# A layer norm's last step moves from ScalarE to POOL, and the negated DFT tables from POOL to ScalarE and VectorE

## The chip, the cores and the metric

The kernel runs on one core of a Trainium2 chip. The metric is device time in microseconds of one execution; the kernel before takes 612.58 us, the median of nine runs that lie between 611.94 and 614.32. A core has five engines that run side by side, each with a queue of its own that it works through in order: TensorE (PE: matmuls; PEld is its loading of weights), VectorE (DVE), ScalarE (ACT), GpSimd (POOL) and SyncE (SP). POOL and SP also issue the transfers (DMAs). An instruction waits at the head of its engine's queue until what it needs is there, and all that stands behind it waits too.

## The reference

Eight batches of attention without softmax (12 heads, 448 positions, 64 columns a head), whose output is the input of a block that mixes with a Fourier transform over positions and columns, normalises, and runs a feed-forward of 768 to 3072 to 768:

```python
scores = scale * np.matmul(q, k.transpose(0, 1, 3, 2))
attn = np.maximum(scores, 0.0) ** 2 / S
x = np.matmul(attn, v)                      # then (B, S, H * D)
X = np.fft.fft(np.fft.fft(x, axis=1), axis=2)
u = x + np.real(X)
un = (u - mean(u)) / np.sqrt(var(u) + 1e-06)     # over the last axis
out = u + np.maximum(un @ w_ch1, 0.0) @ w_ch2
```

## The kernel before

The program writes out every instruction in an order that it plans itself: each piece of work is a generator that yields `need(engine, duration, dependencies, buffers)`, and `Streams.run` (line 79) always takes the piece that could start first by these planned durations. What an instruction is planned to cost, and on which engine, therefore decides the order on all five queues. The hardware then follows that order, with waits on what is really done.

Loading. POOL issues all loads of q, k, v and the weights (lines 306, 335, 345). All matmuls take bf16.

Attention of a batch (line 492): 24 score tiles of 112 x 896 in six groups of four, one group for each pair of heads. A tile's scores are two matmuls (line 544) into one of three double PSUM buffers; ACT takes the relu (line 564) and so frees the buffer; VectorE squares it (line 570); after four tiles TensorE multiplies them with v (line 530, eight matmuls, called the attention values here). `fold` (line 445) copies the result to `xT` (lines 451 to 458) and makes its sum and difference with its mirror image (lines 466, 467). In the start one of the three double PSUM buffers is held for batch 0's channel transform.

Tables. `build_dft` (line 250) makes cosine and sine tables in the first 25 us: VectorE works out a fraction of a turn in three operations (lines 256 to 258, in `turns`), and ACT takes the sine (line 262, in `sine`). `seq` is the table over positions, `chan` three tables over columns. Batch 0 also needs negated ones: `nseq`, the negative of the sine half of `seq`, and `chan_neg`, of a part of each `chan`. `negate` (line 244) makes these four on POOL, planned for 18 us or later.

Start. Batch 0 has no feed-forward beside it. Its channel transform (`first_channels`, line 951, matmuls in line 963) waits in the plan for the folds, the tables and all four `negs_ready`. In the gaps TensorE gets fillers on a tile of zeros (line 1136, `warming`). After the last fold come the copy in line 1000, batch 0's position transform (line 611, where `nseq` is used), its norm and the first feed-forward.

From batch 1 on, three streams are interleaved: the feed-forward of one batch (line 1096 with a relu on ACT in line 1069, then line 1114 with an add on VectorE in line 1077), the attention of a later one, and the mix between them. The position matmuls of a mix (line 838) come in two chunks of rows. `mix_rows` (line 830) handles a chunk: a copy on ACT (line 844), sum and difference on VectorE (line 849), two tiles `u`, one on POOL and one on VectorE (lines 858, 859), their storing, statistics on VectorE (lines 870, 871), a root on ACT (line 874), `rstd` and `nmr` on VectorE (lines 877, 879), and for each of the two tiles `un` = `u` x `rstd` + `nmr` on ACT (line 884). From batch 2 on `un` is stored to DRAM, one tile by SP (`ntop`, line 903) and one by POOL (`nbot`, line 906), and read back transposed (line 929, `unT`) for the feed-forward. So a batch has four `un`, and the six batches from 2 on have 24.

Of the kernel before, what the change touches and what calls it, by code (L numbers as in the profile page):

```python
# [113 lines left out]
def need(eng, dur, deps=(), bufs=(), ok=None):  # L114
    return eng, dur, list(deps), list(bufs), ok
# [6 lines left out]
def act(n):  # L122
    return n / 1200 + 0.2
# [14 lines left out]
def kernel(  # L138
# [24 lines left out]
    SX = 240  # L163
# [75 lines left out]
    chan_neg = work.tile([128, 3, 2, KH], BF16, name="channeg", tag="xn", bufs=1)  # L239
    dft_ready, indices_ready = Cell(), Cell()  # L240

    negs_ready = [Cell() for _ in range(4)]

    def negate(dst, src, t):

        e = yield need("POOL", 0.55, [t, 18.0])
        nc.gpsimd.tensor_scalar(dst, src, -1.0, None, op0=ALU.mult)
        [c for c in negs_ready if c.t is None][0].t = e + LATENCY["POOL"]

    def build_dft():  # L250
        row, col, col2 = drow, dcol, dcol2

        def turns(f, g, cols, rows, n, i):

            r = work.tile([128, 2 * KH], mybir.dt.int32, name="dftr", tag=f"pc{TC[i][0]}", bufs=1)
            nc.vector.tensor_scalar(r[:, :n], cols, rows, None, op0=ALU.mult)
            nc.vector.scalar_tensor_tensor(f, cols, rows, r[:, :n], op0=ALU.mult, op1=ALU.subtract)
            nc.vector.scalar_tensor_tensor(g, f, -1.0, f, op0=ALU.mult, op1=ALU.max)

        def sine(dst, y, n, e, sign=1, bias=zero_t):  # L260
            e = yield need("ACT", act(n), [e + LATENCY["DVE"]])
            nc.scalar.activation(dst, y, AF.Sin, bias=bias, scale=sign * 2.0 * math.pi)
            dft_ready.t = e + LATENCY["ACT"]

        e = yield need("DVE", 0.3, [indices_ready])
        nc.vector.tensor_scalar(row[:, 0:2], row[:, 0:2], 1.0 / S, None, op0=ALU.mult)
        nc.vector.tensor_scalar(row[:, 4:7], row[:, 4:7], 1.0 / D, None, op0=ALU.mult)

        e = yield need("DVE", 2.1, [indices_ready])
        f = work.tile([128, 4 * KH], FP32, name="dfty", tag="u", bufs=2)  # L270
        g = work.tile([128, 4 * KH], FP32, name="dfty", tag="u", bufs=2)
        for i in range(2):
            turns(f[:, i * SX:(i + 1) * SX], g[:, i * SX:(i + 1) * SX], col[:, 0:SX], row[:, i:i + 1], SX, i)
        yield from sine(seq[:, 0, :, :].rearrange("p a s -> p (a s)"), g[:, :2 * SX], 2 * SX, e, -1, halfpi)
        yield from sine(seq[:, 1, :, :].rearrange("p a s -> p (a s)"), f[:, :2 * SX], 2 * SX, e)
        sch.add(negate(nseq, seq[:, 1], dft_ready.t), (1, 1))

        for m in range(3):
            e = yield need("DVE", 1.5, [indices_ready])
            y = work.tile([128, 4 * KH], FP32, name="dfty", tag="u1" if m < 2 else "o", bufs=2)  # L280
            turns(y[:, 2 * KH:], y[:, 0:2 * KH], col2, row[:, 4 + m:5 + m], 2 * KH, m % 2)
            yield from sine(chan[m][:, 0, :], y[:, 0:2 * KH], 2 * KH, e, -1, halfpi)
            yield from sine(chan[m][:, 1, :], y[:, 2 * KH:], 2 * KH, e)
            sch.add(negate(chan_neg[:, m], chan[m][:, :, KH:], dft_ready.t), (1, 1))


    GRP = 4 * R * HG * Dh * 4
# [542 lines left out]
    def mix_rows(b, ch, pcs):  # L830
# [48 lines left out]
        nc.vector.scalar_tensor_tensor(nmr[:n], mv[:n, :, 0], -1.0, rstd[:n],  # L879
                                       op0=ALU.mult, op1=ALU.mult)  # L880
        for i, u in enumerate(us):
            e = yield need("ACT", act(D), [e + (LATENCY["DVE"] if i == 0 else 0.0)])
            un = work.tile([128, D], BF16, name="un", tag=f"un{2 * ch + i}", bufs=1)
            nc.scalar.activation(un[:n], u[:n], AF.Identity, bias=nmr[:n, i:i + 1],  # L884
                                 scale=rstd[:n, i:i + 1])
            uns[b][2 * ch + i] = un
            freed[i].t = e
            if b == 1:
                nr, idn, c0, w = ((128, ident, 64, 128), (128, rev[:, 0:127], 64 + HS + 97, 127),
                                 (96, ident[:96, :96], 64 + 128, 96), (97, rev[:97, 31:128], 64 + HS, 97))[2 * ch + i]  # L890
                sch.add(turn_rows(un, e + 1.5, nr, idn, c0, w, ("DVE", "ACT")[i],
                                  second_un[1 + 2 * ch + i]), (1, 1))
# [58 lines left out]
    def first_channels(i, ms):  # L951

        n0, n1 = TC[i]
        for m in ms:
            e = yield need("PE", 4 * mm(KH), [f_ready[m], dft_ready] + negs_ready + ([first_scores] if i else []),
                           [BS] if i and m == 0 else [])
            if i and m == 0:
                first_pps[i] = BS.take()
            for t in range(2):
                parts = [(0, 2 * KH, chan[m][:, t, :])] if m < 3 else \  # L960
                    [(0, KH, chan[m - 3][:, t, 0:KH]), (KH, 2 * KH, chan_neg[:, m - 3, t, :])]
                for c0, c1, tab in parts:
                    nc.tensor.matmul(first_pps[i][:n1 - n0, t, c0:c1], lhsT=first_folds[m][:, t, n0:n1], rhs=tab,  # L963
                                     start=(i == 1 and m == 0), stop=(m == MC - 1 and c1 == 2 * KH))
# [221 lines left out]
```

## Time and profile before

| | |
|---|---|
| median of nine runs | 612.58 us (611.94 to 614.32) |
| profiled execution, its own time | 614.71 us |
| its span, first to last instruction | 612.7 us |
| mean granted TensorE clock | 0.994 |
| TensorE busy in 0 to 60 us | 53.65 us |
| TensorE busy in 60 to 612.7 us | 545.95 us |
| POOL line 247, nseq / chan_neg | 1.83 / 1.19 to 1.22 us |
| ACT line 884, un, mean of 28 | 1.02 us |
| POOL line 688, the same step for two tiles of batch 0 | 0.98 us |

A line of a timeline gives the start in us, the time in us, the engine, the source line, the operation, what it writes and reads with shapes, how many instructions were merged, and in brackets how long the engine had been idle before and what ended that. A line of the busy table gives a stretch and the busy time of PE, PEld, DVE, ACT and POOL in it with their counts, then the granted TensorE clock, the DMA share and GB/s. In the row of slices each digit is one fortieth of the span, in tenths.

### The profile page before, as it was taken

How to read it: one execution, taken by the hardware profiler on the slowest of the kernel's cores; microseconds unless marked ns; L12 is line 12 of the kernel's file. 1: busy time of each engine (PE TensorE's matmuls, PEld its weight loads, DVE VectorE, ACT ScalarE, POOL GpSimd, SP SyncE). 2: the span in 40 equal slices, each digit the busy share in tenths (PEclk: the TensorE clock that was granted, in tenths of full speed). 3: DMA queues.
4: the chain of work that ended last, by engine and by line, in shares of the span. 5: the costliest groups of instructions: out<-in, count | busy, mean ns of one | idle time of the engine just before them, and what ended most of it. 6: DMA issues, size and time to landing. Idle time of an engine off the chain costs nothing.

```text
span 612.7 us, 10252 instructions
## 1 busy us (share of the span) xinstructions
PE 599.6 (98%) x4048; PEld 331.3 (54%) x4067; DVE 333.3 (54%) x764; ACT 315.6 (52%) x469; POOL 132.4 (22%) x179
## 2 busy tenths in 40 slices
PE   9898999999999999999999999999999999999997
PEld 6556555644455565555445555555445565554464
DVE  6967686864677769545743468645733447110011
ACT  5656763387646468535773167634781346104300
POOL 8823031420242115211420114210410004000000
PEclk9889999999999999999999999999999999999999
DMA  9999999956947994987475774887462225420022
GB/s 125 207 197 200 225 174 127 183 122 110 141 109 182 206 166 160 156 169 122 158 136 105 147 125 158 160 155 116 135 136 70 86 50 170 98 102 26 0 78 78
DMA packets 125216, 82.22 MB, mean 134 GB/s; under 512 B 76272, under 2 KB 113168, under 8 KB 125168
## 3 DMA queue, kind: packets, MB, share of 16 engines
q0 software_dynamic: 40320, 34.07, 35.9%
q1 hardware_dynamic: 84848, 47.50, 31.9%
q8 instruction: 32, 0.52, 0.4%
q14 instruction: 16, 0.13, 0.1%
HBM read 62.91 MB, written 26.69 MB: 146 GB/s over the span
## 4 chain that ended last, share of the span: by engine, by line
PE 86%; DVE 6%; ACT 4%; issue 1%; DMA 1%; POOL 0%; SPq 0%; DVEq 0%; ACTq 0%; POOLq 0%
PE psF L1114 36%; PE psF L1096 32%; PE psS L544 7%; PE psF L530 7%; PE psS L988 2%; ACT sq L564 2%; DMA qkT<-qkr 1%; PE psS L838 1%; ACT un L884 1%; DVE sq L570 1%; PE psS L963 1%; PE psS L1136 1%; DVE stats L870 1%; ACT hT L1069 0%; DVE stats L635 0%
## 5 line engine op out<-in xcount | busy, mean ns | idle before, releaser
L1096 PE MATMUL psF<-unT,w 128*128 128x384 bf16 (+1 forms) x1134 | 227.5, 352 | 2.2 <-ACT hT L1069 1.1
L564 ACT ACTIVATE sq<-psS 112x896 bf16<-112x896 f32 x192 | 165.5, 916 | 118.5 <-PE psS L544 118.5
L1114 PE MATMUL psF<-w,hT 128*128 128x384 bf16 (+2 forms) x1343 | 224.8, 326 | 0.1
L1114 PEld LDWEIGHTS <-hT 128*128 128x128 bf16 x1344 | 129.3, 98 | 92.4 <-issue 8.8
L1096 PEld LDWEIGHTS <-w 128*128 128x128 bf16 x1152 | 109.3, 98 | 111.1 <-issue 14.7
L1069 ACT ACTIVATE hT<-psF 128x512 bf16<-128x512 f32 (+1 forms) x180 | 98.3, 548 | 97.3 <-PE psF L1096 96.3
L570 DVE TENSOR_TENSOR sq<-sq 112x896 bf16<-112x896 bf16 x192 | 117.0, 624 | 49.9 <-ACT sq L564 48.3
L1077 DVE TENSOR_TENSOR o<-psF,o 128x384 f32<-128x384 f32 (+2 forms) x56 | 31.0, 554 | 108.9 <-PE psF L1114 108.4
L451 DVE TENSOR_SCALAR xT<-psF 128x224 bf16<-128x224 f32 x48 | 18.7, 391 | 75.4 <-PE psF L530 71.1
L544 PE MATMUL psS<-qkT 64*112 64x448 bf16 x384 | 53.4, 371 | 1.3 <-ACT sq L564 1.2
L306 POOL DMA_DIRECT2D vn<-in_v_dram x24 | 17.2, 719 | 172.1 <-PE psF L530 153.9
L530 PE MATMUL psF<-sq,vn 112*64 112x448 bf16 x384 | 46.2, 363 | 0.7 <-ACT hT L1069 0.5
L858 POOL TENSOR_TENSOR u<-tp,xn 128x385 f32<-128x385 f32 (+1 forms) x14 | 17.3, 1237 | 105.1 <-DVE tp L849 91.6
L544 PEld LDWEIGHTS <-qkT 64*112 64x112 bf16 x384 | 20.9, 126 | 28.9 <-issue 24.4
L884 ACT ACTIVATE un<-u,nmr,rstd 128x768 bf16<-128x768 f32 (+1 forms) x28 | 28.2, 1021 | 6.7 <-DVE nmr L879 5.6
L530 PEld LDWEIGHTS <-vn 112*64 112x64 bf16 x384 | 18.3, 110 | 22.9 <-issue 14.5
L870 DVE BATCH_NORM_STATS2 stats<-u 128x6 f32<-128x384 f32 (+1 forms) x56 | 28.1, 539 | 0.0
L906 POOL DMA_INDIRECT ubot<-u,back x16 | 16.4, 1028 | 39.6 <-DVE hT L1067 25.0
L1136 PE MATMUL psS<-warm 128*128 128x126 bf16 (+1 forms) x214 | 20.1, 248 | 1.3 <-DVE warm L215 1.3
L306 POOL DMA_DIRECT2D qn<-in_q_dram x21 | 15.4, 732 | 27.3 <-PE psF L427 11.0
L906 POOL DMA_INDIRECT nbot<-un,back x12 | 11.7, 975 | 38.0 <-ACT un L884 34.3
L1136 PEld LDWEIGHTS <-warm 128*128 128x128 bf16 x214 | 14.7, 111 | 7.0 <-issue 5.1
(119 smaller groups left out, 371.9 us busy)
## 6 DMA issues: line engine op xcount, KB each, us to landing
out_dram<-o SPq DMA_DIRECT2D x27, 384.0 KB, 2.3
vn<-in_v_dram POOLq DMA_DIRECT2D x24, 224.0 KB, 5.2
qn<-in_q_dram POOLq DMA_DIRECT2D x21, 224.0 KB, 6.4
kn<-in_k_dram POOLq DMA_DIRECT2D x21, 224.0 KB, 7.2
w<-in_moe_w_ch_dram POOLq DMA_DIRECT2D x12, 384.0 KB, 11.6
w<-in_moe_w_ch_dram POOLq DMA_DIRECT2D x4, 1152.0 KB, 25.0
utop<-u SPq DMA_DIRECT2D x8, 384.0 KB
o<-utop SPq DMA_DIRECT2D x8, 384.0 KB, 3.6
```

Of the source, the lines that this page charges most:

```text
L306: nc.gpsimd.dma_start(out=t, in_=src[b, hs].rearrange("h (p j) d -> p h (j d)", j=4))
L530: nc.tensor.matmul(av[h * Dh:(h + 1) * Dh, 0:S], lhsT=vn[:, c, h0 + h, :], rhs=sq[:, h, :], start=(c == 0), stop=(c == 3))
L544: nc.tensor.matmul(sc[:R, h, 0:S].rearrange("k (c q) -> k c q", c=4), lhsT=kT[ps, m % 2, c, :], rhs=qT[ps, m % 2], start=True, stop=True)
L564: nc.scalar.activation(r, sc[:R, :, 0:S], AF.Relu)
L570: nc.vector.tensor_tensor(r, r, r, op=ALU.mult)
L870: nc.vector.bn_stats(stats[:n, hf, :], u[:n, hf * (D // 2):(hf + 1) * (D // 2)])
L884: nc.scalar.activation(un[:n], u[:n], AF.Identity, bias=nmr[:n, i:i + 1], scale=rstd[:n, i:i + 1])
L1069: nc.scalar.activation(h[:, 0:N], ph[:, 0:N], AF.Relu)
L1077: nc.vector.tensor_tensor(o[:, hs], pc[:, 0:w], o[:, hs], op=ALU.add)
L1096: nc.tensor.matmul(ph[:, 0:N], lhsT=w1_sb[m][hf][:, jj * 128:(jj + 1) * 128], rhs=unT[:, m, 0:N], start=(m == 0), stop=(m == MC - 1))
L1114: nc.tensor.matmul(pc[:, 0:w], lhsT=hT[j][:, c * 128:(c + 1) * 128], rhs=w2_sb[j // 6][:, j % 6, hs], start=(j == 0), stop=(j == JC - 1))
L1136: nc.tensor.matmul(first_pps[0][:, t, c0:512], lhsT=warm[:, 0:128], rhs=warm[:, c0:512], start=not begun, stop=False)
```

## The change

Two edits. From batch 2 on `un` is one instruction on POOL in place of one on ACT, planned at 1.05 us. And POOL's four negations go: `nseq` comes from a third sine on ACT with a negative scale, `chan_neg` from a negation on VectorE behind each pair of sines; `first_channels` no longer waits for `negs_ready`. Since the plan changes, instructions near both places stand in another order too.

```diff
-    negs_ready = [Cell() for _ in range(4)]
-
-    def negate(dst, src, t):
-
-        e = yield need("POOL", 0.55, [t, 18.0])
-        nc.gpsimd.tensor_scalar(dst, src, -1.0, None, op0=ALU.mult)
-        [c for c in negs_ready if c.t is None][0].t = e + LATENCY["POOL"]
-
...
-        sch.add(negate(nseq, seq[:, 1], dft_ready.t), (1, 1))
+        yield from sine(nseq.rearrange("p a s -> p (a s)"), f[:, :2 * SX], 2 * SX, e, -1)
...
-            sch.add(negate(chan_neg[:, m], chan[m][:, :, KH:], dft_ready.t), (1, 1))
+            e = yield need("DVE", 0.3, [dft_ready])
+            nc.vector.tensor_scalar(chan_neg[:, m], chan[m][:, :, KH:], -1.0, None, op0=ALU.mult)
+            dft_ready.t = e + LATENCY["DVE"]
...
-            e = yield need("ACT", act(D), [e + (LATENCY["DVE"] if i == 0 else 0.0)])
+
+            en = "POOL" if b > 1 else "ACT"
+            e = yield need(en, act(D) if b == 1 else 1.05, [e + (LATENCY["DVE"] if i == 0 else 0.0)])
             un = work.tile([128, D], BF16, name="un", tag=f"un{2 * ch + i}", bufs=1)
-            nc.scalar.activation(un[:n], u[:n], AF.Identity, bias=nmr[:n, i:i + 1],
-                                 scale=rstd[:n, i:i + 1])
+            if b > 1:
+                nc.gpsimd.tensor_scalar(un[:n], u[:n], rstd[:n, i:i + 1], nmr[:n, i:i + 1],
+                                        op0=ALU.mult, op1=ALU.add)
+            else:
+                nc.scalar.activation(un[:n], u[:n], AF.Identity, bias=nmr[:n, i:i + 1],
+                                     scale=rstd[:n, i:i + 1])
...
-            e = yield need("PE", 4 * mm(KH), [f_ready[m], dft_ready] + negs_ready + ([first_scores] if i else []),
+            e = yield need("PE", 4 * mm(KH), [f_ready[m], dft_ready] + ([first_scores] if i else []),
                            [BS] if i and m == 0 else [])
```

## The prediction

> **What bounds the kernel now.** I read the page first (busy shares, the 40 slices), then the busy table of single stretches, then the timelines of TensorE, VectorE, GpSimd (POOL) and ScalarE (ACT) where TensorE was not busy at full clock.
>
> ```profile
> PE 599.6 (98%) x4048; PEld 331.3 (54%) x4067; DVE 333.3 (54%) x764; ACT 315.6 (52%) x469; POOL 132.4 (22%) x179
> ...
> PEclk9889999999999999999999999999999999999999
> ```
>
> TensorE is busy for 98% of the 612.7 us span, and runs at full clock except in slices 1 to 3. It does the same work after the change, so time can only move where it idles, runs slowly, or runs fillers (the matmuls on `warm`). The busy table, asked for 0 to 60 us and the rest, gives TensorE 53.65 of 60.00 and 545.95 of 552.70: half of the idle time lies in the first tenth. There the chain of waits goes through ACT squares, VectorE squares and the making of the tables. The table of three stretches (PE, PEld, DVE, ACT, POOL busy; then clock, DMA share, GB/s):
>
> ```profile
> 23.49:26.90 3.41, 1.81 (x25) 1.09 (x22) 3.31 (x9) 3.04 (x5) 3.41 (x6) 1.00 1.08 212
> 26.90:33.73 6.83, 6.83 (x37) 2.99 (x36) 4.45 (x10) 3.86 (x5) 1.56 (x3) 0.50 1.09 214
> 54.21:57.62 3.41, 2.09 (x34) 1.75 (x32) 2.48 (x10) 2.85 (x5) 1.16 (x2) 1.00 1.15 250
> ```
>
> A stretch of 3.41 us with TensorE 53% busy is followed by 6.83 us at half clock; one that is 61% busy (the third) is not. What empties the first, from the timelines:
>
> ```profile
> 18.15 1.83 POOL L247 TENSOR_SCALAR nseq<-seqm 128x480 bf16<-128x480 bf16 x1
> ...
> 18.09 1.54 DVE L570 TENSOR_TENSOR sq<-sq 112x896 bf16<-112x896 bf16 x2
> ...
> 20.09 1.71 DVE L570 TENSOR_TENSOR sq<-sq 112x896 bf16<-112x896 bf16 x2
> ...
> 22.91 0.92 DVE L258 SCALAR_TENSOR_TENSOR dfty<-dfty 128x386 f32<-128x386 f32 x1
> ...
> 24.48 0.58 PE L427 MATMUL psF<-ident,qk 112*64 112x112 bf16 x16 [0.83 <-DVE xT L458]
> ...
> 25.84 0.40 PE L544 MATMUL psS<-qkT 64*112 64x448 bf16 x2 [0.77 <-ACT sq L564]
> ...
> 26.93 1.70 PE L530 MATMUL psF<-sq,vn 112*64 112x448 bf16 x8
> ...
> 33.75 0.95 PE L530 MATMUL psF<-sq,vn 112*64 112x448 bf16 x8
> ```
>
> While POOL negates, two squares on VectorE take 1.54 and 1.71 us in place of 1.24, and line 258 takes 0.92 in place of 0.56: 1.1 us lost, just before the last table. TensorE then waits 0.83 and 0.77 us, and the clock halves: line 530 takes 1.70 us where it takes 0.95 later. The other stalls that the change can reach are relus (line 1069) queued behind the norm's last step (line 884) on ACT:
>
> ```profile
> 236.48 1.03 ACT L884 ACTIVATE un<-u,nmr,rstd 128x768 bf16<-128x768 f32 x1 [0.20 <-DVE nmr L879]
> ...
> 239.93 2.11 PE L1096 MATMUL psF<-unT,w 128*128 128x384 bf16 x12 [0.44 <-ACT hT L1069]
> ...
> 515.42 6.09 PE L1096 MATMUL psF<-unT,w 128*128 128x384 bf16 x36 [0.54 <-ACT hT L1069]
> 521.67 2.11 PE L1096 MATMUL psF<-unT,w 128*128 128x384 bf16 x12 [0.16 <-ACT hT L1069]
> ```
>
> **Part 1, the tables.** Removed: four POOL negations (1.83 and three of 1.19 to 1.22, 5.5 us), and the planned wait of the first channel matmuls for them. Eight load issues of w1 move up past them by as much; the DMA share stays above 1.0 from 10 to 60 us, so I cost that at nothing (without that cover, w1 would come earlier, a gain). Added: one more sine of 480 columns on ACT, 0.60 us (8.22 minus 7.62), and three negations of 386 bf16 columns on VectorE. No row shows those; the folds (two inputs, 225 columns) take 0.28, line 256 (fp32, 386 columns) 0.42, so each lies between 0.2 and 0.42. I take 0.3, nearer the bf16 row.
>
> The planner also reorders the start, so I followed the new order by hand with the old durations:
> - ACT: third sine to 9.5; squares 0 to 3 to 12.85 (0.81 apart); chan0's two sines to 13.9; the qkT copy, which stood before the squares, to 14.75. Squares 4 and 5 end at 16.85. Before, square 6 ended at 16.9, so ACT is 0.8 behind here.
> - VectorE: its first negation waits for chan0's sine (13.95); behind it in the queue are the three operations of chan1, which end at 15.9 (before 17.0). ACT goes through chan1's sines without a wait (16.85 to 17.9) and on to square 10 (22.6).
> - VectorE, undisturbed, ends chan2's three operations at 22.9 (before 23.84). Square 11 starts at 23.4 (before 24.89), and the third attention-value group (line 530) at 25.55 (before 26.93): **1.4 us won**.
> - TensorE's gaps in this order: 0.75 us before scores 4 and 5 (the late qkT copy), 0.35 after, 0.4 near 18.5, 0.5 for fold 1, 0.3. No 3.41 us hold more than 1.1 us of them, so the worst stretch is 68% busy, above the 61% that kept full clock. From the third to the fourth such group, 6.82 us at half clock (26.93 to 33.75) become 3.85 (25.55 to 29.4, set by squares 14 and 15 at 0.81 each and the fold between): **3.0 us won**.
> - To the end of batch 0's channel matmuls: four of these (0.09 each) and four fillers (0.055 each) leave the path, as the order has them where it waits for the last fold: **0.6 us won**.
>
> What follows (line 1000 to the first feed-forward matmul, 45.6 to 59.8) is the same chain, so the sum stands: 5.0 us. The bound below: all my gaps close less well and the clock drops anyway, 0 to 1.4 won, less 0.6 + 3 x 0.42 = 1.9 if the new operations all lie on the path, a loss of up to 1.9.
>
> The rule beside this row is in the Trainium skill, "TensorE: Matmul & The Clock Gate", section "What's actually happening": the clock is halved after about 3.4 us of too little matmul work, in windows that run free of the kernel. The trace agrees in length (6.83 us is two windows). By the rule the two gaps fall into one window only in some executions, which would put the median's loss below the profile's.
>
> **Part 2, the norm.** 24 instructions of 1.02 us (four in each of six batches) leave ACT; 24 of 0.98 (line 688, the same form on POOL, 51.69 us) join POOL, which is 22% busy. Two lie between the second u and its store on POOL, so that store comes some 2 us later, and two between the two stores of nbot. In POOL's queue the last pair also stands ahead of the next load of v; that load waited 4.44 us for line 530 in batch 2, 4.11 in 3 and 5, 2.21 in 4, so two instructions of 0.98 fit and I cost them at nothing (uncovered, a load would be up to 2 us late). In batch 2, SP's queue now has the second ntop store behind one xn transpose and both unT transposes behind two (1.2 us each): the second unT transpose was issued at 198.70, taking 4.28, and its feed-forward begins at 214.8, so over 10 us cover it. On ACT the stalls of 0.44, 0.54 and 0.16 can go: **1.1 us won** at most. What is late next is VectorE: in batch 3 the attention values start at 241.97, with the last square only just done.
>
> The price is on VectorE: a two-input operation meets a POOL one. In batch 3, line 879 takes 0.91 us in place of 0.16 while POOL runs line 858, so 0.75 to 0.98 per meeting. Most of the 24 fall on the statistics (line 870, 0.5 us each whether POOL works or not). The places without room: batch 2, where the order now puts the values 18 matmuls sooner (near 186.1; the needed square by about 185.9), and batches 3 and 5, whose second pair falls on folds and squares. I take 0.5 + 0.25 + 0.25 = 1.0 lost; the bounds are 0, and 0.98 in each of the five batches with attention beside them, 4.9. Net of part 2: 0.1 won.
>
> The Trainium skill, "SBUF — State Buffer", section "SBUF: two separate sides", speaks against this part: the port pair that VectorE and GpSimd share is locked for a whole instruction and the loser blocks. The 0.91 beside 0.16 agrees. By the rule every meeting costs up to 0.98, which as a bound gives 613.5; by the row of idle TensorE time it gives 609.6.
>
> **The sum.** The profiled execution took 614.71 (span 612.7 and 2.0 around it), 2.13 above the median of 612.58; one of the nine runs, 614.32, stands near it. 614.71 - 5.0 - 0.1 = **609.6**. I read the 2.13 as the half-clock stretch, which the median then lacks; against the median the change wins 3.0.
>
> **The rivals.**
> - A, 0.48: as above, 609.6 (608.2 to 611.4).
> - B, 0.10: the half clock is in every run and the 2.13 is the profiler's. Then 612.58 - 5.1 = 607.5. For it: the nine runs show no clear second group; against it: 614.32.
> - C, 0.15: no gain that shows. The clock drops in the new order, at the 0.75 and 0.35 us gaps near 14 to 16.5, and gives back 3.0: 612.6. Or the tables were never on the path; against that stands the chain of waits, which passes through lines 258 and 262 at 22.9 to 25.0.
> - D, 0.27, slower: POOL's norm holds up VectorE's squares ahead of the attention values. At 4.9 in place of 1.0 the time is 613.5, and with the start's bound (half of the 5.0 won) 616.0; I put it at 614.5. It decides from 3.0 + 1.2 = 4.2 us of new TensorE waits on. For it: batch 3's values follow their square with no room; against it: in batch 4 the square ends 3.3 us before line 530 starts.
>
> **How the numbers follow.** A measurement of this kernel can tell about 0.2% (1.2 us) from no change. A and B are faster, 0.58; C the same, 0.15; D slower, 0.27. The predicted time is A's. The range 607.0 to 614.6 leaves out the tail of B and the upper half of D, about 0.2.
>
> **What would show it.** Right: clock 1.00 in all slices, or no stretch at 0.50 near 27 to 34; batch 0's line 1000 near 40 in place of 45.6; the first feed-forward matmul near 54.5 in place of 59.8; squares of 0.62 us at 18 to 23; no relu wait near 240 and 515; from there on every stage shifted by the same amount. Wrong: a half-clock stretch between 15 and 30; TensorE waiting on VectorE squares at line 530 in batches 2 to 6; POOL's un above 1.5 us; unT landing after its feed-forward's first matmul could start. The prediction falls if the start wins under 2 us, or if part 2 adds waits of over 2.

## The result, and the profile after

The changed kernel takes 609.52 us (median of 20 runs, 608.21 to 611.77) where the kernel before takes 613.18 us (62 runs, 611.06 to 615.91): a ratio of 0.9938, 95% interval 0.9927 to 0.9948, or 3.7 us. Forecast were 609.6 us and "faster". The profiled execution took 608.22 us with a span of 606.4, against 614.71 and 612.7: between the two profiles 6.5 us went, not 3.7. Executions of one kernel differ here by up to 5 us and more (one further execution of the changed kernel on record, beside the 20, took 612.85 at a granted clock of 0.997), so a profile says what can happen in an execution, and the median what usually does. Much of what follows is about that difference.

From the page of the changed kernel, the row of TensorE and the row of the granted clock:

```profile
PE 595.1 (98%) x4044; PEld 329.1 (54%) x4063; DVE 337.4 (56%) x767; ACT 294.9 (49%) x446; POOL 154.0 (25%) x199
...
PEclk9999999999999999999999999999999999999999
```

No slice is under full clock any more. POOL has 21.6 us more, ACT 20.7 less. The busy table of the changed kernel, first tenth and rest:

```profile
0.00:60.00 60.00, 54.18 (x642) 36.82 (x643) 44.13 (x110) 41.15 (x60) 30.00 (x66) 1.00 1.14 192
60.00:606.40 546.40, 540.91 (x3404) 292.24 (x3421) 293.25 (x658) 253.72 (x387) 124.04 (x133) 1.00 0.65 129
```

The clock of the first 60 us is 1.00 in place of 0.94, which the same row of the kernel before has:

```profile
0.00:60.00 60.00, 53.65 (x605) 36.53 (x606) 42.63 (x101) 37.63 (x54) 35.99 (x70) 0.94 1.12 182
```

TensorE's timeline in the start of the changed kernel (line 524 is the former 530, 605 the former 611, 710 the former 716):

```profile
20.57 0.95 PE L524 MATMUL psF<-sq,vn 112*64 112x448 bf16 x8
25.15 0.95 PE L524 MATMUL psF<-sq,vn 112*64 112x448 bf16 x8
29.24 0.95 PE L524 MATMUL psF<-sq,vn 112*64 112x448 bf16 x8
...
41.81 0.66 PE L605 MATMUL psS<-pc,seqm 128*128 128x384 bf16 x2 [0.78 <-ACT pc L1000]
...
51.45 0.49 PE L710 MATMUL psS<-warm 128*128 128x256 bf16 x3 [0.73 <-ACT unT L737]
53.13 0.49 PE L710 MATMUL psF<-warm 128*128 128x256 bf16 x3 [0.94 <-DVE unT L737]
...
54.90 1.15 PE L1096 MATMUL psF<-unT,w 128*128 128x384 bf16 x6
```

The two last of these moments in the kernel before:

```profile
46.65 0.66 PE L611 MATMUL psS<-pc,seqm 128*128 128x384 bf16 x2 [0.78 <-ACT pc L1000]
...
59.75 1.15 PE L1096 MATMUL psF<-unT,w 128*128 128x384 bf16 x6
```

The third group of attention values starts at 25.15 (before 26.93), the fourth at 29.24 (33.75), the position matmuls at 41.81 (46.65), the first feed-forward at 54.90 (59.75). So the start wins 4.85 us. VectorE and POOL of the changed kernel, the rows in question:

```profile
18.40 1.69 DVE L564 TENSOR_TENSOR sq<-sq 112x896 bf16<-112x896 bf16 x3
...
20.01 0.26 DVE L277 TENSOR_SCALAR channeg<-chan 128x386 bf16<-128x386 bf16 x1
...
L881 POOL TENSOR_SCALAR un<-u,rstd,nmr x24: 971/972/1602, 177.6 to 515.6; 128x768 bf16<-128x768 f32 x12, 112x768 bf16<-112x768 f32 x12
```

Three squares in 1.69 us, where two took 1.54 and 1.71 beside POOL's negation; the new negation is 0.26. The last line is the answer on the tile `un`: shortest, median and longest of the 24 steps on POOL in ns. Six of the 24 took 1.35 to 1.60 us, so their mean is 1.10. From the first feed-forward to the end of the last instruction the changed kernel needs 551.54 us, the kernel before 552.91: another 1.4 won. (Of the 6.5 us between the two profiled times 0.3 stands outside the span.) The three waits for a relu (0.44, 0.54, 0.16) are gone, and no square holds up line 524.

### The profile page after: what moved, and what is told of

The parts are those of the page before. It is cut to its first block, busy times and chain, and to the rows that moved or that the text cites. A ratio compares the mean times of both kernels' runs of the same rounds, so it can differ in the third digit from the quotient of the medians.

```text
span 606.4 us, 10238 instructions
## 1 busy us (share of the span) xinstructions
PE 595.1 (98%) x4044; PEld 329.1 (54%) x4063; DVE 337.4 (56%) x767; ACT 294.9 (49%) x446; POOL 154.0 (25%) x199
## 4 chain that ended last, share of the span: by engine, by line
PE 57%; DVE 4%; ACT 1%; issue 0%; DVEq 0%; ACTq 0%
PE psF L1114 27%; PE psF L1096 21%; PE psF L524 3%; PE psS L538 3%; PE psS L988 1%; DVE stats L864 1%; ACT sq L558 1%; PE psS L832 1%; DVE u L853 1%; DVE sq L564 1%; ACT hT L1069 0%; DVE u L852 0%; DVE nmr L873 0%; DVE tm L843 0%; DVE mv L865 0%
## 5 line engine op out<-in xcount | busy, mean ns | idle before, releaser
L445 DVE TENSOR_SCALAR xT<-psF 128x224 bf16<-128x224 f32 x48 | 18.7, 390 | 68.3 <-PE psF L524 68.3
L881 POOL TENSOR_SCALAR un<-u,rstd,nmr 128x768 bf16<-128x768 f32 (+1 forms) x24 | 26.3, 1099 | 6.0 <-DVE nmr L873 5.6
L1136 PE MATMUL psS<-warm 128*128 128x126 bf16 (+1 forms) x210 | 18.0, 234 | 1.3 <-DVE warm L215 1.3
L460 DVE TENSOR_TENSOR fold<-xT 128x225 bf16<-128x225 bf16 x48 | 17.4, 362 | 2.5 <-ACT xT L450 0.5
L452 DVE TENSOR_SCALAR xT<-psF 128x224 bf16<-128x224 f32 x47 | 18.0, 384 | 0.0
```

Source lines behind the costliest of these rows:

```text
L445: nc.vector.tensor_scalar(x[:, 0:HS].rearrange("q (p j) -> q p j", j=4), at[:, 0:R // 2], 1.0 / (64.0 * S), None, op0=ALU.mult)
L881: nc.gpsimd.tensor_scalar(un[:n], u[:n], rstd[:n, i:i + 1], nmr[:n, i:i + 1], op0=ALU.mult, op1=ALU.add)
```

## The experiments

The same few moments are compared in every profile: the position matmul of batch 0, the first feed-forward, and the first channel matmul (line 988, shifted where the listing is) of batches 1, 2, ... . From that of batch 1 to the end is called the rest, from that of batch 2 to that of batch 3 the stretch of batch 2.

### The two parts, one at a time

The tables alone: the norm stays on ACT.

```diff
-            en = "POOL" if b > 1 else "ACT"
-            e = yield need(en, act(D) if b == 1 else 1.05, [e + (LATENCY["DVE"] if i == 0 else 0.0)])
+            e = yield need("ACT", act(D), [e + (LATENCY["DVE"] if i == 0 else 0.0)])
...
+            nc.scalar.activation(un[:n], u[:n], AF.Identity, bias=nmr[:n, i:i + 1],
+                                 scale=rstd[:n, i:i + 1])
```

> Part 1 alone: the negations leave POOL, the norm's last step stays on ScalarE. My theory (the start is the gain): the first feed-forward matmul stands near 54.9 us as with both parts, and the late relu waits of 0.44, 0.54 and 0.16 us near 235 and 510 us are there again; the profiled time lies 4.9 to 5.1 us under the kernel before, 1.1 to 1.4 over the whole change. Rival (the gain needs the norm on POOL): under 2 us won.

The norm alone: the kernel before, with POOL's step from batch 2 on.

```diff
-            e = yield need("ACT", act(D), [e + (LATENCY["DVE"] if i == 0 else 0.0)])
+            en = "POOL" if b > 1 else "ACT"
+            e = yield need(en, act(D) if b == 1 else 1.05, [e + (LATENCY["DVE"] if i == 0 else 0.0)])
...
+            if b > 1:
+                nc.gpsimd.tensor_scalar(un[:n], u[:n], rstd[:n, i:i + 1], nmr[:n, i:i + 1],
+                                        op0=ALU.mult, op1=ALU.add)
```

> Part 2 alone: the norm's last step on POOL from batch 2, the tables still negated by POOL. My theory: the start is as before (first feed-forward matmul at 59.8 us, a stretch of 6.8 us at half clock in the profile), and the rest wins 1.1 to 1.4 us because no relu waits behind the norm. Rival (VectorE is held up by POOL at the port): 0 to 4.9 us slower than before.

Measured, beside 29 runs of the kernel before on the same chip (median 612.94): the tables alone 612.93, ratio 0.9988 (0.9964 to 1.0013); the norm alone 613.10, ratio 0.9993 (0.9975 to 1.0012). By the medians neither part does anything, and both together win 3.7 in the result's runs. The profiles say more. Tables alone: position matmul at 41.89, first feed-forward at 55.65 (a wait of 0.64 for POOL's `un` in batch 0's norm, in TensorE's timeline), the rest 509.3 us as in the kernel before (509.1), all three relu waits back. Norm alone: the start ends nearly where it did before (46.04, 59.52), the rest takes 508.05. That the start is as late as before is in part chance: the stretch of 6.8 us at half clock that was expected is not there (the fourth group of attention values, at 33.15, follows the third after 3.93 us), and a wait that has nothing to do with either part makes up for it, in TensorE's timeline:

```profile
15.02 0.39 PE L427 MATMUL psF<-ident,qk 112*64 112x112 bf16 x8 [1.97 <-DMA qk<-in_k_dram]
```

The load of k for the second group landed 1.97 us late; in the changed kernel's profile that wait is 0.20. So the gains stand in the profiles where the prediction put them, the tables' in the start and the norm's in the rest; in the medians they don't show. Something in the executions is worth as much as a part of the change. The granted clock, which every run records, is one such thing: 20 of those 29 runs of the kernel before were at 0.999 or more (median 612.55), 9 at 0.997 or less (614.39). Of the tables alone 7 of 12 were at 0.999 or more (median 610.64), of the norm alone 5 of 12 (611.71). So where the clock held, the tables were 1.9 us and the norm 0.8 us faster than the kernel before; the medians hide that, as the clock held in fewer runs of the parts than of the kernel before. Why it did is open.

### The half clock taken away by fillers

The kernel before, with 27 more matmuls on the tile of zeros where the third group of heads is turned and before score tile 13, that is in the stretch that was 53% busy:

```diff
+    def fill(n):
+        for _ in range(n):
+            nc.tensor.matmul(first_pps[0][:, 0, 2 * KH:512], lhsT=warm[:, 0:128], rhs=warm[:, 2 * KH:512],
+                             start=False, stop=False)
...
+                if b == 0 and g == 2 and r == 1 and x == 0:
+                    fill(14)
...
+                if b == 0 and i == 13:
+                    fill(13)
```

> The kernel before with 27 more filler matmuls (14 ahead of the transposes of group 2, 13 ahead of score tile 13), in the two gaps of 0.83 and 0.77 us; nothing else is moved. Theory that the half clock costs 3.0 us: no stretch at 0.50, line 530's third group takes 0.95 us in place of 1.70, batch 0's line 1000 comes near 42.6 in place of 45.6, profiled time near 611.7, and the median 1 to 3 us under the kernel before. Rival (the start is bound by ScalarE and VectorE and the clock costs nothing): line 1000 stays at 45.6 and the median is the same.

The profile has no half clock, and TensorE's timeline shows the position matmul at

```profile
43.62 0.66 PE L620 MATMUL psS<-pc,seqm 128*128 128x384 bf16 x2 [0.78 <-ACT pc L1009]
```

in place of 46.65: the half clock was 3.0 us of the profiled execution, as the prediction had it. But the median is 613.54, ratio 1.0009 (0.9990 to 1.0029): no gain. Most runs of the kernel before have no half clock to lose, and in the 8 of 12 runs whose clock held the fillers' median is 613.43, 0.9 over that of the kernel before. That fits the prediction's reading of the 2.13 us between profile and median. But 4 of the 12 were still at 0.997 or less, about as large a share as without the fillers (9 of 29): these two gaps are not the only place that can halve the clock.

### The kernel before, once more

> The kernel before once more, for another profile of it. 14 in 20 of its runs so far had a granted clock of 0.999 or more, so most likely this shows its start at full clock. Theory (the half clock was 3.0 of the 4.9 us won between the two first profiles): third attention-value group at 26 to 27, fourth 3.9 to 4.2 after it (6.8 when halved), position matmul at 43.3 to 44.2, span 609.5 to 611. Rival (half clock or not, the start stays as late because other waits end it): position matmul within 1 us of 46.65.

It came out at a clock of 0.997, in 614.44 us. The busy table of that execution in steps of 3.41 us, and TensorE:

```profile
22.70:26.11 3.41, 1.81 (x32) 1.34 (x28) 3.27 (x9) 2.35 (x4) 3.38 (x6) 0.97 1.08 211
26.11:29.52 3.41, 3.41 (x15) 1.14 (x14) 2.34 (x5) 1.19 (x2) 1.71 (x3) 0.52 1.07 211
29.52:32.93 3.41, 3.41 (x36) 1.86 (x34) 2.80 (x7) 3.25 (x4) 0.53 (x1) 1.00 1.08 212
```

```profile
24.38 0.58 PE L427 MATMUL psF<-ident,qk 112*64 112x112 bf16 x16 [0.83 <-DVE xT L458]
25.74 0.47 PE L544 MATMUL psS<-qkT 64*112 64x448 bf16 x2 [0.77 <-ACT sq L564]
...
27.54 1.71 PE L530 MATMUL psF<-sq,vn 112*64 112x448 bf16 x8
...
32.29 0.95 PE L530 MATMUL psF<-sq,vn 112*64 112x448 bf16 x8
```

The same two gaps (0.83, 0.77), the same 53% busy, and this time the clock is halved for one stretch of 3.41 us, not for two (these rows begin 0.17 us after the clock's own stretches, hence 0.97 and 0.52 in place of 1.00 and 0.50). The position matmul comes at 45.18, between the 46.65 of two such stretches and the 43.62 of none. A mean clock of 0.997 is one stretch (half of 3.41 us is 0.28% of the span), 0.994 two; it does not tell where they stood. The norm alone has the same start, and the third outcome (TensorE, then the busy table):

```profile
26.77 0.58 PE L427 MATMUL psF<-ident,qk 112*64 112x112 bf16 x16 [0.84 <-DVE xT L458]
28.13 0.40 PE L544 MATMUL psS<-qkT 64*112 64x448 bf16 x2 [0.77 <-ACT sq L564]
...
29.22 0.95 PE L530 MATMUL psF<-sq,vn 112*64 112x448 bf16 x8
```

```profile
24.30:27.71 3.41, 2.22 (x39) 1.72 (x37) 3.24 (x8) 1.99 (x4) 3.39 (x6) 1.00 1.05 199
```

The gaps are there and the clock holds. So they are in the order of the instructions, and what they cost is 0, 1.5 or 3.0 us by execution. The traces record the moments at which the granted clock changes. In each of the 14 traces all of them lie whole multiples of 3.41 us apart (in the third look at the tables alone, below, 6.99, 54.77, 58.19, 204.96 and 208.37), but at another place in each execution: stretches that the work does not shift. On its own stretches the kernel before is 53% busy from 23.49 and from 22.53 in its two profiles, with both gaps in one stretch. In the norm alone an edge at 27.71 cuts the second gap, and the stretch ahead of it is 65% busy. The page "TensorE: Matmul & The Clock Gate" of the Trainium skill, section "What's actually happening", has the windows run free of the kernel; one and the same gap with three outcomes agrees with that. The page has the clock halved after an idle window; here one that was 53% busy was enough. Why the half clock lasts for one stretch or for two is not shown.

### What slowed VectorE in the start

The kernel before, POOL's negations replaced by filling the tables with zero (the negation itself is left out, all waits and the order stay):

```diff
-        nc.gpsimd.tensor_scalar(dst, src, -1.0, None, op0=ALU.mult)
+        nc.gpsimd.memset(dst, 0.0)
```

> The kernel before, with POOL's four negations replaced by filling the same tables with zero: the negation is left out, so that POOL reads nothing for them while order and waits stay as they were. It tells what it was in the negations that slowed VectorE. If reading and writing on POOL beside VectorE's two-input operations is the cause: the squares at 18 to 22 us at 0.62 each in place of 0.77 and 0.86, line 258 of the last table at 0.56 in place of 0.92, the third attention-value group 0.8 to 1.1 us earlier than 26.9, no stretch at half clock, line 1000 at 41.5 to 43. If the squares are slow for another reason (ACT or the DMAs beside them), they stay at 0.77 and 0.86 with a POOL that only fills, and line 1000 comes at 43 to 46.

VectorE's timeline, then TensorE's, of this kernel:

```profile
17.88 1.15 DVE L570 TENSOR_TENSOR sq<-sq 112x896 bf16<-112x896 bf16 x2
...
19.48 1.15 DVE L570 TENSOR_TENSOR sq<-sq 112x896 bf16<-112x896 bf16 x2
...
21.66 0.56 DVE L258 SCALAR_TENSOR_TENSOR dfty<-dfty 128x386 f32<-128x386 f32 x1
```

```profile
25.33 0.95 PE L530 MATMUL psF<-sq,vn 112*64 112x448 bf16 x8
29.25 0.95 PE L530 MATMUL psF<-sq,vn 112*64 112x448 bf16 x8
...
42.15 0.66 PE L611 MATMUL psS<-pc,seqm 128*128 128x384 bf16 x2 [0.78 <-ACT pc L1000]
```

Two squares take 1.15 us in place of 1.54 and 1.71, line 258 takes 0.56 in place of 0.92, the gap of 0.83 is gone and so is the half clock. ACT and the DMAs work beside the squares here as they did before, so neither was the cause; it was POOL's negations beside VectorE. What in them is less clear: the fills are shorter too (0.44 to 0.66 us in place of 1.19 to 1.83), and only 0.26 us of one lay beside these four squares. The few operations of VectorE that a fill did meet were not longer (0.62 each for a square and for line 257), so that reading is the cause is likely, on little overlap. This one execution took 610.36 us, 2.1 less than the median of the kernel before at full clock on that chip (612.43). With the position matmul as the mark, the 4.8 us of the start are now told apart: 46.65 to 43.62 is the half clock, 43.62 to 42.15 the meetings of POOL and VectorE (0.2 us of which stands ahead of the first negation and is chance), and 0.3 us, to 41.81, is left for the new order, the sine and the negations between them. The tables alone had the mark at 41.76 to 42.19 in three executions, so that 0.3 is not told from nothing.

### The price of the norm on POOL

The changed kernel, each of the 24 moved steps done twice:

```diff
+                for _ in range(2):
+                    nc.gpsimd.tensor_scalar(un[:n], u[:n], rstd[:n, i:i + 1], nmr[:n, i:i + 1],
+                                            op0=ALU.mult, op1=ALU.add)
```

> The changed kernel with each of the 24 steps that moved to POOL done twice there (the second time with the same result): 24 more instructions of 0.97 us on POOL, beside VectorE's. It doubles the port meetings that the prediction priced at 1.0 us and the rival in which POOL's norm holds up VectorE at 4.9. Theory (the meetings fall where VectorE has room; the changed kernel's TensorE waits nowhere for a square that they delayed): from batch 1's mix to the end, 507.7 us in the changed kernel, at most 1 us more. By the prediction's price: 1.0 us more. By the rival's: 4 to 5 us more, as waits of TensorE for VectorE's squares or for POOL's un in batches 2 to 6.

The rest takes 510.1 us, 2.4 more than in the changed kernel: between the two theories' figures. But 1.7 of it is in one place, the stretch of batch 2 (57.37 in place of 55.66), VectorE and TensorE there:

```profile
214.61 0.49 DVE L389 COPY qkr<-kn 112x1024 bf16<-112x1024 bf16 x1 [2.71 <-DMA qkT<-qkr]
```

```profile
216.49 1.15 PE L1097 MATMUL psF<-unT,w 128*128 128x384 bf16 x6 [1.53 <-DVE xT L452]
```

That is a wait of VectorE for a transfer, and none for a square that POOL held up. Another 0.4 is in the stretch of batch 3 (62.49 in place of 62.07). From batch 4's channel matmuls on, where 16 of the doubled steps are, the whole costs 0.2 us (327.05 in place of 326.82). So from batch 4 on the meetings that the prediction priced are worth next to nothing; POOL's lateness in batch 2 may be worth more, through the transfers behind it. One execution doesn't tell that from the variation that the next run shows.

### The parts again, with the whole beside them

On another chip, with the kernel before at 613.29 there:

> The changed kernel once more, as the yardstick of the three runs beside it. Theory (the gain is the start's, and it is there in the median too): 3.0 to 4.0 us under the kernel before, most executions at a granted clock of 0.999 or more, first feed-forward matmul of batch 0 at 54.5 to 55.5, the stretch from there to the end 551.3 to 551.7 us. Rival (the gain measured first was the chip's or the day's): under 2 us.

> The tables' part alone once more (the norm's last step back on ACT). If the two parts add up as their traces say, this is 1.1 to 1.5 us over the whole change and 1.8 to 2.5 us under the kernel before. Rival: the parts do not add up, and the tables alone again win nothing in the median (within 0.7 us of the kernel before), 3 us over the whole change; then something in the start differs between the two although its code is the same. The place to look: the first feed-forward matmul of batch 0, 54.9 in the whole change and 55.65 in the first run of this part alone.

> The tables' part alone a third time, for a profile of one of its slower executions. On two chips 11 of 24 of its runs had a granted clock of 0.997 or less, against 6 of 28 of the whole change's, and its median lay 0.6 us from the kernel before. If the loss is in the start, the stretch from batch 1's mix to the end is 509.1 to 509.4 again, and what is above a span of 607.8 stands before that, as a stretch at half clock or a late load. If it is in the end, that stretch grows. At a clock of 0.999 or more this run tells little: 607.8 to 609 and the same milestones as in the second run.

The whole change 608.54, ratio 0.9918 (0.9895 to 0.9941), all six runs at full clock. Its profile needs 552.0 us from the first feed-forward on, more than expected: in batch 3 TensorE waits 0.41 us at 236.55 for the norm's root, as it did not in the first profile. The tables alone 611.82, ratio 0.9987 (0.9969 to 1.0006), seven of twelve runs below 0.999 (with those of the first comparison 12 of 24; the expectation of the next run counts one too few). Its profiled execution (span 607.8) is at full clock and has the same start as the whole change, first feed-forward at 54.86 against 54.92, and the same moments up to batch 2; what it lacks is 0.97 us behind batch 7's channel matmuls (111.02 against 110.05), where the relu waits were. Its five runs at 0.999 or more have a median of 611.24, those of the kernel before on this chip 612.43: 1.2 us won where the clock held.

The third look at the tables alone took 617.62 us, eight more than the second, and the loss is mostly at a place not looked at until then. Its rest is 515.1, six more than the 509.1 of the second; all of that lies in the stretch of batch 2, 62.73 us in place of 56.75. SP, VectorE and TensorE of that execution:

```profile
193.50 1.32 SPq L398 DMA_TRANSPOSE qkT<-qkr  x1
194.99 4.30 SPq L923 DMA_TRANSPOSE unT<-ntop  x1
199.40 4.53 SPq L923 DMA_TRANSPOSE unT<-nbot  x1
```

```profile
203.17 0.43 DVE L389 COPY qkr<-kn 112x1024 bf16<-112x1024 bf16 x1 [6.57 <-DMA qkT<-qkr]
```

```profile
204.25 3.37 PE L1108 MATMUL psF<-w,hT 128*128 128x384 bf16 x12 [4.17 <-DVE xT L452]
```

VectorE copies q and k of a group of heads into `qkr`, which has a single buffer, for SP to transpose. The transpose of the last k, issued at 193.50, landed 9.6 us later (the longest of the transfers of that tile), while three loads of 224 KB that POOL issued from 193.0 on and the transposes of `unT` were under way. VectorE stood at the next copy for 6.57 us, all its other work behind it, and TensorE ran dry for 4.17. Then the clock halved (from 204.96 to 208.37), which makes up the rest of the six.

The wait is no accident of that one run. In seven profiles with `un` on ACT (both of the kernel before, the two that vary it, three of the tables alone) VectorE waits at this copy in five, for 1.30, 1.66, 1.54, 2.38 and 6.57 us, and TensorE loses 0 to 0.18 us in five of the seven, 1.25 in the second look at the kernel before, and 4.17 here. The changed order has the transpose of k 2.7 and 3.5 us ahead of the next loads of q and k (1.3 and 2.0 in the first profile of the kernel before, 0.3 and 1.0 in the third look at the tables alone), and the first of the two `unT` transposes some four us later (196.38, and 191.87 in the second look at the tables alone, whose start is the same). SP of the changed kernel:

```profile
187.93 1.66 SPq L398 DMA_TRANSPOSE qkT<-qkr  x1
190.98 0.53 SPq L903 DMA_DIRECT2D ntop<-un  x1
196.38 1.73 SPq L929 DMA_TRANSPOSE unT<-ntop  x1
198.21 1.31 SPq L929 DMA_TRANSPOSE unT<-nbot  x1
```

The two `unT` transposes take 1.73 and 1.31 there, not 4.30 and 4.53, and in none of the five executions of the changed order (the two of the whole change, the norm alone, and two variants that touch only the start) does TensorE wait at that place. VectorE does wait at this copy in all five, mostly one or two groups later, for 0.33 to 3.06 us, and in one of them TensorE loses 0.28 us to it. The doubled steps above and a variant below lose 1.53 and 4.94 us one group later. So a loss of over 1 us stands in two of seven traces with `un` on ACT and in two of seven with it on POOL, though these last two were altered further. That the new order lessens the risk, and that the norm's part does more in the median than the 0.9 to 1.4 us it wins in a profile without that wait, is possible and not shown.

There is a second place where the clock can halve, and both kernels have it: the end of batch 0's norm, where TensorE waits 0.73 and 0.94 us. The busy table of the third look at the tables alone, then of the first profile of the whole change, each on the stretches of its own clock:

```profile
51.36:54.77 3.41, 1.70 (x25) 1.45 (x24) 2.18 (x7) 2.19 (x5) 0.01 (x1) 1.00 1.17 229
54.77:58.18 3.41, 3.10 (x24) 1.67 (x24) 2.20 (x5) 1.08 (x4) 0.00 (x0) 0.50 1.24 206
```

```profile
49.06:52.47 3.41, 2.40 (x37) 2.04 (x35) 2.48 (x9) 2.77 (x6) 1.44 (x2) 1.00 1.14 264
52.47:55.88 3.41, 2.43 (x37) 1.82 (x36) 2.48 (x7) 1.56 (x4) 0.00 (x0) 1.00 1.24 206
```

The same code: in the one both waits fall into one stretch, which is 50% busy, and the clock halves behind it; in the other an edge at 52.47 cuts the second wait, the two stretches are 70 and 71% busy, and it holds. The norm alone halves here too (from 58.43, behind a stretch 49% busy), and so does the last variant below (from 54.99, behind 50%). The busy share does not decide it alone: it held behind 51% in the second look at the kernel before (from 53.24), behind 52% in the second look at the tables alone (from 49.62) and behind 53% in the doubled steps (from 49.66). So a run at 0.997 may have lost its stretch here or in the first gaps, and its clock does not say which.

### Three tries at a better kernel

More fillers at that second place (6 and 8 more behind the waits for `unT`):

```diff
-        yield from turn(2, 3)
+        yield from turn(2, 9)
...
-        yield from turn(3, 3)
+        yield from turn(3, 11)
```

> The changed kernel with 6 and 8 more filler matmuls of 256 columns ahead of the last two batches of transposes of batch 0's norm (0.7 and 0.9 us, where TensorE waits 0.73 and 0.94 us). Theory that the changed kernel's slower runs (granted clock 0.997) lose a 3.4 us window to the gaps there: no run under 0.999, median near 608.5, 1.0 under the change. Rival (the loss sits elsewhere, or the runs differ for another reason): the median stays near 609.5 or rises by the fillers' own 0.1 to 0.3 us.

All six runs were at full clock, with a median of 609.13 and a ratio of 0.9929 (0.9902 to 0.9957), against 609.52 and 0.9938 without: no difference to be told. The first feed-forward came 14.2 us after the position matmul, 1.1 later than without, and one wait of 1.3 us for a relu stands in its trace, so what the clock can cost in some executions the fillers cost in all.

The loads of batch 0 in another order, to take out the wait for q and k of the second group; the index patterns of the tables are made earlier, and a channel matmul waits in the plan for its own table alone:

```diff
-        for i in range(NG):
-            yield from load_group(i)
+        for i, which in ((0, (0, 1)), (1, (0, 1)), (0, (2,)), (1, (2,)), (2, (0, 1, 2))):
+            yield from load_group(i, which)
...
-            e = yield need("PE", 4 * mm(KH), [f_ready[m], dft_ready] + ([first_scores] if i else []),
+            e = yield need("PE", 4 * mm(KH), [f_ready[m], chan_ready[m % 3]] + ([first_scores] if i else []),
```

> The changed kernel with the loads of batch 0 in another order: q and k of the second group of heads ahead of the values, and the index patterns of the tables made after the first two loads. If the differences of 2 to 3 us between executions at full clock come from a load of q or k of the second group that lands late (a wait of 1.97 us for one stood in the run of the norm's part alone, 0.20 in the changed kernel), the executions at full clock draw together (spread under 1.2 us), and the median is 0.3 to 1.0 us below the changed kernel's. If they come from elsewhere, the spread stays at 2 to 3 us and the median within 0.3 us of it. A price on the other side: the values land later, by some 1.5 us, against a first attention-value matmul at 16.2; if they are needed there, the first group starts late by as much.

610.08, ratio 0.9944 (0.9924 to 0.9964), 1.5 slower than the changed kernel beside it; the spread is 0.5 us in seven runs, but there it was 0.6 in six, so what the late load does to the spread stays open. The first four groups of attention values came up to 2.3 us earlier (26.94 for the fourth, 29.24 in the changed kernel), the fifth only at 33.86: the copy of transposed q and k that it needs stood on VectorE behind the last table. With those copies first:

```diff
-        sch.add(turning(), (2, 2))
+        sch.add(turning(), (2, 0.4))
```

> The kernel with the reordered loads (whose first four attention-value groups came at 14.3, 18.3, 23.0 and 26.9, up to 2.3 us ahead of the changed kernel, but whose fifth waited until 33.9 for a copy of transposed q and k that stood on VectorE behind the last table), with these copies ahead of the tables in VectorE's order. If that copy alone lost the lead, the fifth group comes at 30.8 to 31.5 (33.3 in the changed kernel), line 1000 at 39.5 to 40.5, and the median is 1.0 to 2.3 us below the changed kernel's. If VectorE's own load sets the start (3.1 to 3.3 us busy in each 3.4 from 14 to 31 us), only the order of the wait changes: line 1000 at 41.5 or later, and a median within 0.7 us of the changed kernel's.

617.99, ratio 1.0080 (1.0067 to 1.0094): slower than the kernel before. The start kept 1.1 us of its lead to the fourth group (28.14), 0.6 to the fifth (32.66) and 0.3 to the position matmul (41.50). Line 1000 comes at 40.43, 40.73 in the changed kernel, so the two readings' marks for it do not tell them apart; the fifth group met neither (30.8 to 31.5, 33.3). VectorE is 3.1 to 3.3 us busy in each 3.4, so that it sets the start is likely. And the edit was wider than meant: the rank holds in all batches. Most of the loss is in batch 2 again, at the place just found, VectorE and TensorE:

```profile
216.43 0.43 DVE L390 COPY qkr<-kn 112x1024 bf16<-112x1024 bf16 x1 [7.71 <-DMA qkT<-qkr]
```

```profile
217.51 5.41 PE L1097 MATMUL psF<-unT,w 128*128 128x384 bf16 x18 [4.94 <-DVE xT L453]
```

with the half clock behind it. All six runs were at 0.994 or less. No version beat the changed kernel.

## Why the prediction was right, and where it was not

It said 609.6 and the median is 609.52. That is closer than its steps deserve: two errors of 1.4 and 1.3 us cancel.

- **The start, 5.0 us won.** Measured 4.85. By its terms: to the third group of attention values 1.78 (said 1.4); from the third to the fourth 2.73 (said 3.0: 4.09 us in place of 6.82, where the forecast had 3.85); from there to the first feed-forward 0.34 (said 0.6; the matmuls and fillers saved hardly mattered). The order followed by hand gave 25.55 and 29.4 for the two groups, and they came at 25.15 and 29.24.
- **The gaps in the new order.** Said were 0.75, 0.35, 0.4, 0.5 and 0.3 us between 14 and 26 us. There is one of 0.20 for a load and one of 0.34, and none after 16.3: VectorE's and ACT's operations stood closer than the hand count. The 0.82 at 10.4 was not in it. That the clock would hold was right.
- **The meetings with the negations.** Said were 1.1 us lost on VectorE, with 1.24 for two squares undisturbed. With the tables filled the two took 1.15, so the loss was 1.3.
- **The prices of the new operations.** Negation 0.3, measured 0.26; the sine 0.60, measured 0.68 by its own duration and 0.58 from start to start; `un` on POOL 0.98, median 0.97, mean 1.10. "POOL's un above 1.5 us" was named as a sign of being wrong: three of the 24 took 1.60, and no wait of TensorE follows from them.
- **Part 2's gain, 1.1 us at most.** The relu waits went. In batches 2 and 3 together that is 0.05 us in one profile of the whole change and 0.5 in the other (118.18 and 117.73, before 118.22); behind batch 7's channel matmuls it is 0.97, where the two waits gone made up 0.70. The profile with only 0.05 has the new wait of 0.41 for the norm's root.
- **Part 2's price, 1.0 us: the step that failed.** It was "0.5 + 0.25 + 0.25" at meetings of VectorE with POOL. In batches 4 to 6 the changed kernel takes 0.1 us longer (216.77 against 216.68, all of it in batch 5, where 0.25 was said), and twice as many steps on POOL cost 0.2 from batch 4 on. VectorE meets POOL, but has the room: the wait of TensorE at line 524 that should follow is not there. So part 2 won 1.4 us in the profile (0.9 between the second profiles of the whole change and of the tables alone), not 0.1, and the profiled execution 6.5 us, not 5.1; what the start and part 2 leave of that, 0.3, stands outside the span.
- **From the profile to the median.** The prediction held that the median lacks the half clock, and counted 3.0 us against it. The three outcomes of the same gaps show that; two thirds of the runs of the kernel before are at full clock. Its reason, that the two gaps fall into one window only in some executions, is what the traces show (an edge at 27.71 cuts the second in the norm alone). It did not ask the same of the changed kernel: its profile, 608.22, lies at the lower end of its executions, 1.3 us below their median. By the lowest run of each the gain is 2.85 us (611.06 to 608.21), and the tables alone have 1.55 of it (609.51), the norm alone 0.4 (610.63, of twelve runs). The 0.8 that the medians show above that would come from executions disturbed less often: 6 of 28 runs of the changed kernel are at a clock under 0.999, 19 of 58 of the kernel before. The kinds of disturbance seen are the first two gaps of the kernel before, a late load (norm alone), the end of batch 0's norm and the copy into `qkr` in batch 2; that they account for it is not shown, nor why the tables alone, with less to go wrong in the start, are under 0.999 in 12 of 24 runs. Even where the clock held, the parts (1.2 to 1.9 and 0.8 us) make less than the whole on the second chip (608.54 against 612.43, 3.9 us). That sum stays open.
- **Part 2's transposes, costed at nothing.** The prediction looked at the second `unT` transpose in batch 2 ("issued at 198.70, taking 4.28") and found over 10 us of cover for its feed-forward. That was right. What it did not ask is who else waits in that queue: the copy of q and k on VectorE, through a buffer that a transpose frees. Whether the move is a gain there is not shown.
- **The rivals.** B (all runs at half clock) is out by the clocks of the runs. C's second mechanism, tables not on the path, is out by the zero fill. D's, squares held up in batches 2 to 6, appears in no profile.

The page "SBUF — State Buffer" of the Trainium skill, section "SBUF: two separate sides", has a port pair that VectorE and GpSimd share, locked for a whole instruction. The start agrees that the two meet (squares 0.77 and 0.86 on average beside a negation, 0.58 without), but not that it is for a whole instruction: the square that ended at 19.63 did so inside the negation of 18.15 to 19.98. In batches 2 to 7 the 0.98 for each meeting that the prediction drew from this was a limit and no estimate.

## What to carry to other kernels

A gap that drops TensorE's busy share to half for some 3.4 us cost 0, 1.5 or 3.0 us here, by where the edges of the clock's stretches fell, so a profile shows one draw; take the granted clocks of several runs before pricing it, and ask the busy table on the stretches of the clock itself. When work is moved between engines, list every single-buffered tile whose freeing transfer changes its place in a DMA queue, and who stands at the head of which queue waiting for it. And parts that do nothing one by one in medians can still add up: look at the profiles' fixed moments and the lowest runs before calling a part idle.

## What the hardware showed that was not expected

- A transpose of 224 KB by DMA took 2.9 to 9.6 us from issue to landing in the same program (third look at the tables alone), and the `unT` pair of batch 2 took 1.25 (norm alone) to 5.34 us each (second look at the kernel before) on SP's queue.
- The clock changed only at moments whole multiples of 3.41 us apart. On these stretches it fell after 49, 50 and 53% busy in some executions and held after 51, 52 and 53% in others, and fell for one or for two stretches after the same gaps.
- With POOL filling the tables, VectorE's squares stayed at 0.58 us, though the fills hardly lay beside them; with POOL negating they took 0.77 to 0.86.
